# Where w_ch2 is converted, who makes w2's high parts, and a first MLP pass over two chunks

## The chip, the core and the metric

The kernel runs on one core of one Trainium2 chip. The metric is device time in microseconds (us), from the first to the last instruction. Lower is better. Three runs of the kernel before gave 1047.99, 1050.70 and 1052.57 us; the median is 1050.7 us.

## The reference, cut to what matters

Three stages follow one another: causal attention with a cumulative bias, a mixture of 8 experts (one expert for each token), and a mixer with a channel MLP. B=4, S=576, so 2304 tokens; the model width DM is 512.

```python
attn_out = _attn_ref(q, k, v, s)                   # 4 x 8 x 576 x 64
# experts: w1 is 8 x 512 x 1024, w2 is 8 x 1024 x 512, float32
h = np.maximum(x[b, s] @ w1[e], 0.0)
out[b, s] = p[e] * (h @ w2[e])
# mixer: U 576 x 32, V 32 x 576, w_ch1 512 x 2048, w_ch2 2048 x 512
h = xt @ U @ V
u = x + h.transpose(0, 2, 1)
ch = np.maximum(u @ w_ch1, 0.0) @ w_ch2
return (u + ch).astype(np.float32)
```

`w_ch1`, `w_ch2`, `U` and `V` arrive as float64. The kernel turns them into float32 on the chip by integer operations on their words.

## The kernel before, in words

Every product is made of three products of float32 parts: a number is split into a high part, which TensorE takes exactly, and a low part, and high by high, high by low and low by high are summed in PSUM. So each weight needs a high part (a cast) and a low part (a subtraction). The helper `conv` (L228) makes both: the high part on the engine it is given (GpSimd at L232, ScalarE at L236), the low part at L239.

The work is staged. Attention and the router come first, in an order written out by hand (`ORDER`); the change touches nothing there. Then come the experts, one after the other, by falling count of tokens, with 384, 384, 368, 336, 320, 304, 256 and 256 rows (`CAPS`); they are called experts 0 to 7 here. The mixer and the MLP come last, over 9 chunks of 256 tokens.

Experts and MLP share the loop `ffn` (L1512). One step f of it holds 12 matmuls of the first product into a PSUM tile `ps_h` (L1524), ScalarE's relu `hh` (L1501) and VectorE's low part `hl` (L1502), and then, `skew` steps late, the second product of an earlier step into `acc` (L1538): 3 matmuls for each 128 tokens. After each step a `hook` issues the work that stands beside the loop. The experts have 8 steps with a skew of 2, so 10 hooks each and 80 in all (NH = 10). The MLP has 16 steps with a skew of 1.

The order of every engine's queue is the order of the program text, so a hook decides what stands in front of what. An expert's hook issues, in this order:
- `mix_step` (L1881): for each tile of 128 rows of the expert before, a cast `yh`, a subtraction `yl` (L1939) and 3 matmuls into `pu` (L1853).
- `run_convs` (L1832): step f converts `w1` unit f of the next expert (high part on ScalarE, low part on VectorE) and `w2` unit f-2 (both parts on GpSimd). The units overwrite a ring of 16 tiles that the present expert still reads, so a unit of `w2` waits for the last `acc` matmul on the old one.
- `load_raws` (L1828): the loads for the hook after next, on SP, into a pool of 5 buffers.
- the rows of the next expert (`load_x` L1757, indirect DMAs on GpSimd; `trans_x` L1773 on TensorE, L1776; `split_x` L1779), and `ug_make` (L1789, GpSimd, L1804).
- one entry of a list `seq` (L1839 to L1848, popped at L1914): the conversions of float64 weights. A unit of 128 x 512 is a 512 KB load on SP, an absolute value on ScalarE (L256), three tensor_scalar on VectorE (L257, L265, L273), two scalar_tensor_tensor on VectorE (L285, L293), and a use. Each unit takes two entries.

`seq` holds 16 units of `w_ch2` first, then 16 of `w_ch1`, then 2 of `V`: 70 entries, one of them before the loop and one in each hook after it. The use of a `w_ch2` unit is a store of its float32 words to DRAM (`c2_d`, L1470). The use of a `w_ch1` unit is the high part on ScalarE (L1455) and the low part on GpSimd (L1456), into tiles that stay. In the hooks of expert 7, where no next expert's weights are due, `run_convs` loads the 16 units of `c2_d` back (`load_c2` L220) and splits them into the ring: 15 with ScalarE and VectorE, one on GpSimd.

After the experts, the last rows are scattered to DRAM (`yt_d`, L1926), and the MLP's first chunk is prepared: its rows are loaded (L2004), the mixer's product is made (`ph`, L2018) and added (L2025), and the sum is transposed (`ups`, L2032) and split into `uh` (L2034) and `ul` (L2035). These PSUM tiles come from a ring of two. The next chunk is prepared inside the loop of the present one: its hooks 8 and 10 make the sums, 11 and 13 the transposes.

Of the kernel before, what the change touches and what calls it, by code (L numbers as in the profile page):

```python
# [12 lines left out]
F32 = mybir.dt.float32  # L13
# [14 lines left out]
# the order of issue of the attention's and the router's jobs  # L28
# [99 lines left out]
def kernel(  # L128
# [37 lines left out]
    # rows that the main path takes of the first expert, then of the others by falling count  # L166
# [19 lines left out]
    # rows of all tokens; those of the first expert by place; what else a place needs  # L186
# [7 lines left out]
    c2_d = dram.tile([F2, DM], F32, name="c2_d")  # L194
# [114 lines left out]
    # ------------------------------------------------------------------  # L309
    # causal attention with the cumulative bias, and the router  # L310
    # ------------------------------------------------------------------
    with ExitStack() as ax:
# [240 lines left out]
        # ---- v as two float16 parts, a column of ones beside each head; the v of a pair of  # L553
        # heads is scaled by a power of two first, by the sum of its magnitudes ----
# [14 lines left out]
        # for each pair of heads: what scales v, and the power of two to undo it  # L569
# [778 lines left out]
        def group_jobs(g):  # L1348
            """Loads of four heads."""
# [91 lines left out]
    # V as its high part twice and its low part, for a product with the parts of U' x stacked  # L1441
# [20 lines left out]
    def c2_job(pool, f):  # L1462
# [6 lines left out]
        def use(t):  # L1469
            nc.sync.dma_start(c2_d[f * P : (f + 1) * P], t)  # L1470
# [41 lines left out]
    def ffn(ps1, psa, hpool, xh, xl, n, u1, u2, nf, skew, hook):  # L1512
        rows = [(i, min(P, n - i * P)) for i in range((n + P - 1) // P)]
        acc = [psa.tile([P, DM], F32, tag=f"acc{i}", name=f"acc{i}") for i, _ in rows]
        done = []
        for f in range(nf + skew):
            if f < nf:
# [3 lines left out]
                ops = [(wh, xh), (wh, xl), (wl, xh)]  # L1521
                for kk in range(KD):
# [211 lines left out]
    with ExitStack() as mx:  # L1734
# [141 lines left out]
        for g_ in seq.pop(0):  # L1876
            g_()
# [252 lines left out]
```

## Time and profile before

| what | value |
|---|---|
| median of 3 runs | 1050.7 us |
| span of the profiled execution | 1056.8 us |
| TensorE busy over the span | 91% |
| VectorE, ScalarE, GpSimd busy | 56%, 38%, 39% |
| mean granted clock of TensorE | 0.952 |
| first matmul of experts 0 to 7 at | 329.2, 366.25, 403.95, 440.96, 477.27, 515.95, 555.79, 592.97 us |
| first matmul of the MLP at | 631.12 us |

The profiled execution's own time is its span, as the page gives it; it is 6.1 us above the median of the timed runs. "Busy" counts the time in which an engine had an instruction under way, and says nothing of whether that instruction was waiting for something inside it. A matmul's end is modelled and matmuls overlap, so the pace of TensorE is read from how many matmuls lie between two points of time, not from their single durations. The granted clock is given in parts of 2.4 GHz.

### The profile page before, as it was taken

The numbers are of one execution on the slowest core, as the hardware profiler recorded it, in microseconds if no ns is written. First come the engines' busy times: TensorE is split into PE (matmuls) and PEld (weight loads), VectorE is DVE, ScalarE is ACT, GpSimd is POOL, SyncE is SP. The second block draws the span as 40 slices with busy tenths as digits, with TensorE's granted clock in tenths as the row PEclk, the third lists the DMA queues.
The fourth block names the chain that finished last, engine by engine and source line by source line (L and its number), as shares of the span: only waits on it lengthen the run. The fifth ranks groups of instructions, "written<-read, shape, count | busy, mean of one in ns | idle before, by whom it ended". The sixth has DMA issues, their size and how long they took to land.

```text
span 1056.8 us, 19123 instructions
## 1 busy us (share of the span) xinstructions
PE 964.1 (91%) x7139; PEld 853.1 (81%) x7139; DVE 590.3 (56%) x1136; ACT 406.6 (38%) x960; POOL 410.3 (39%) x508
## 2 busy tenths in 40 slices
PE   5888998889847999998897879999999999999998
PEld 4777887778746988887686759999999999999997
DVE  6676887767745888989999851222222222222221
ACT  4676877777622334435444341111111111111111
POOL 6633636355643877889999920000000000000000
PEclk9898999999956999999998989999999999999999
DMA  7998998967126697677575450101010100101000
GB/s 171 196 204 158 233 216 209 213 134 177 35 73 192 223 309 246 211 258 220 172 214 179 135 181 1 35 6 41 1 40 1 40 21 21 40 1 41 1 20 20
DMA packets 132132, 129.25 MB, mean 122 GB/s; under 512 B 59015, under 2 KB 100295, under 8 KB 130240
## 3 DMA queue, kind: packets, MB, share of 16 engines
q1 hardware_dynamic: 123968, 114.03, 40.0%
q0 software_dynamic: 6864, 13.63, 4.4%
q8 instruction: 58, 0.95, 0.4%
q10 hardware_dynamic: 1200, 0.30, 0.1%
q14 instruction: 42, 0.34, 0.1%
HBM read 81.04 MB, written 26.49 MB: 102 GB/s over the span
## 4 chain that ended last, share of the span: by engine, by line
PE 59%; POOL 13%; DMA 8%; DVE 7%; issue 6%; SPq 4%; ACT 3%; POOLq 0%; DVEq 0%; ACTq 0%
PE ps_h L1524 24%; PE acc L1538 22%; POOL ring L239 4%; DMA OP<-parts 3%; PE pp L779 3%; POOL ring L232 2%; POOL c1u L1456 2%; SPq L541 2%; PE ob L828 2%; PE sm L1012 1%; PE sp L709 1%; PE sp L716 1%; POOL ug L1804 1%; DMA OP<-b_d 1%; POOL yt_d L1926 1%
## 5 line engine op out<-in xcount | busy, mean ns | idle before, releaser
L1538 PE MATMUL acc<-ring,hh 128*128 128x512 f32 x928 | 291.6, 395 | 0.0
L1502 DVE SCALAR_TENSOR_TENSOR hl<-ps_h,hh 128x256 fp32r<-128x256 f32 (+5 forms) x208 | 92.3, 444 | 288.7 <-ACT hh L1501 285.7
L1501 ACT ACTIVATE hh<-ps_h 128x256 fp32r<-128x256 f32 (+5 forms) x208 | 83.3, 400 | 415.8 <-PE ps_h L1524 400.8
L1524 PE MATMUL ps_h<-uh,c1u 128*128 128x256 f32 x1152 | 232.1, 286 | 0.7 <-ACT uh L2034 0.7
L1524 PEld LDWEIGHTS ps_h<-uh,c1u 128*128 128x128 f32 x1152 | 190.0, 192 | 6.1 <-ACT uh L2034 1.1
L1538 PE MATMUL acc<-ring,hl 128*128 128x512 f32 (+4 forms) x464 | 181.7, 392 | 1.9 <-DVE hl L1502 1.9
L1538 PEld LDWEIGHTS acc<-ring,hh 128*128 128x128 f32 x928 | 161.1, 187 | 25.8
L1524 PE MATMUL ps_h<-ul,c1u 128*128 128x256 f32 x576 | 164.1, 285 | 0.1
L1524 PE MATMUL ps_h<-xh,ring 128*128 128x384 f32 (+5 forms) x512 | 128.1, 322 | 2.8 <-DVE hl L1502 2.2
L1524 PEld LDWEIGHTS ps_h<-ul,c1u 128*128 128x128 f32 x576 | 110.9, 193 | 5.1 <-DVE ul L2035 0.4
L1538 PEld LDWEIGHTS acc<-ring,hl 128*128 128x128 f32 (+4 forms) x464 | 85.9, 185 | 24.1 <-DVE hl L1502 2.7
L792 DVE SCALAR_TENSOR_TENSOR lo<-pp,hi 128x384 f16<-128x384 f32 (+2 forms) x160 | 85.3, 549 | 24.7 <-ACT hi L787 19.6
L1524 PEld LDWEIGHTS ps_h<-xh,ring 128*128 128x128 f32 x512 | 92.8, 197 | 6.6 <-DVE hl L1502 2.8
L239 POOL TENSOR_TENSOR ring<-raw_out,ring 128x512 fp32r<-128x512 f32 x60 | 88.2, 1470 | 5.0
L779 PE MATMUL pp<-ident,Pb 128*128 128x128 f32 x480 | 83.9, 297 | 6.1 <-DVE lo L792 2.3
L787 ACT ACTIVATE hi<-pp 128x384 f16<-128x384 f32 (+2 forms) x160 | 77.0, 496 | 32.1 <-PE pp L779 25.2
L1524 PE MATMUL ps_h<-xl,ring 128*128 128x384 f32 (+5 forms) x256 | 82.3, 322 | 1.6 <-DVE xl L1782 1.5
L750 ACT ACTIVATE Pb<-sp,nm 128x192 f32<-128x192 f32 (+4 forms) x160 | 80.8, 535 | 6.8 <-DVE nm L733 5.7
L709 PE MATMUL sp<-OP 128*128 128x288 f32 (+4 forms) x192 | 71.6, 377 | 8.5 <-DMA OP<-parts 2.8
L733 DVE TENSOR_REDUCE nm<-sp 128x1 f32<-128x576 f32 (+4 forms) x96 | 67.5, 703 | 15.9 <-PE sp L724 13.8
L828 PE MATMUL ob<-VP,hi 128*128 128x65 f16 x960 | 59.1, 199 | 5.8 <-ACT xr L840 5.7
L716 PE MATMUL sp<-OP 68*128 68x288 f32 (+4 forms) x192 | 60.7, 321 | 2.8 <-DMA OP<-b_d 2.8
(228 smaller groups left out, 1579.7 us busy)
## 6 DMA issues: line engine op xcount, KB each, us to landing
raw_in<-in_moe_w_dram SPq DMA_DIRECT2D x64, 256.0 KB
raw_out<-in_moe_w_dram SPq DMA_DIRECT2D x64, 256.0 KB
raw<-in_moe_w_ch_dram SPq DMA_DIRECT2D x32, 512.0 KB
OP<-parts SPq DMA_DIRECT2D x28, 576.0 KB
OP<-parts SPq DMA_DIRECT2D x28, 288.0 KB
out_dram<-ut SPq DMA_DIRECT2D x9, 512.0 KB
kn<-in_k_dram SPq DMA_DIRECT2D x32, 128.0 KB
x_d<-x SPq DMA_DIRECT2D x16, 256.0 KB
```

What stands on the lines that cost most here:

```text
L239: lo_eng.tensor_tensor(out=lo, in0=src, in1=hi.bitcast(F32), op=ALU.subtract)
L709: nc.tensor.matmul(sp[:, c, :cw], lhsT=W1[j][:, h, t * P : (t + 1) * P], rhs=K1[j][:, h, c0 : c0 + cw], start=True, stop=False,)
L716: nc.tensor.matmul(sp[:, c, :cw], lhsT=W2[j][0:SK, h, t * P : (t + 1) * P], rhs=K2[j][0:SK, h, c0 : c0 + cw], start=False, stop=not diag,)
L750: nc.scalar.activation(out_, in_, AF.Exp, scale=-1.0, bias=k["nm"][:, x : x + 1])
L779: nc.tensor.transpose(pp[:, i - i0], k["pb"][:, a, x * P : (x + 1) * P], ident)
L787: nc.scalar.activation(k["hi"][:, i0:i1], k["pp", i0][:, : i1 - i0], AF.Copy, scale=SCALE)
L792: nc.vector.scalar_tensor_tensor(out=k["lo"][:, i0:i1], in0=k["pp", i0][:, : i1 - i0], scalar=SCALE, in1=k["hi"][:, i0:i1], op0=ALU.mult, ...
L828: nc.tensor.matmul(o[:, h], lhsT=pt[:, a * (t + 1) + x], rhs=VP[n % 2][:, z, x, h], start=(x == 0 and i == 0), stop=(x == t and i == len(t ...
L1501: nc.scalar.activation(hh[:, :n], ps[:, :n], AF.Relu)
L1502: nc.vector.scalar_tensor_tensor(out=hl[:, :n], in0=ps[:, :n], scalar=0.0, in1=hh[:, :n].bitcast(F32), op0=ALU.max, op1=ALU.subtract,)
L1524: nc.tensor.matmul(ps[:, :n], lhsT=wa[:, kk], rhs=xa[:, kk, :n], start=(kk == 0 and i == 0), stop=(kk == KD - 1 and i == 2),)
L1538: nc.tensor.matmul(acc[i][0:m], lhsT=ha[:, sl], rhs=u2[g][:, wa], start=(g == 0 and jj == 0), stop=(g == nf - 1 and jj == 2),)
```

## The change

What it does:
- The store to `c2_d` and the loads back are gone. A unit of `w_ch2` is now split straight from the converted words (high part on ScalarE, low part on GpSimd).
- The `w_ch2` units leave the experts' list. `seq` holds 16 units of `w_ch1` and 2 of `V`: one entry before the loop, and 37 spread evenly over the first 68 hooks, all within experts 0 to 6. The list of `w_ch2` has 34 entries: one in each of the 10 hooks of expert 7, and then two in each hook of the MLP's first pass until it is empty.
- The high parts of `w2` for experts 1 to 7 go from GpSimd to ScalarE. Their low parts stay on GpSimd.
- The MLP's first pass takes two chunks (512 tokens): each step makes 24 matmuls of 256 columns into one `ps_h` tile, one relu and one `hl` of 512 columns, and 12 `acc` matmuls. Both chunks are prepared ahead of the pass. The other 7 chunks run as before.
- Buffers: the conversions' tiles are in a pool of their own that outlives the experts, `mixb` is in the pool of raw weights, `ut`, `uh` and `ul` have 3 buffers for 2, and `hh` and `hl` have skew + 1 buffers.

The diff, without the comments that it drops:

```diff
-    c2_d = dram.tile([F2, DM], F32, name="c2_d")
...
-    def load_c2(f):
-        raw = wraw.tile([P, DM], F32, tag="raw", name="raw_c2")
-        nc.sync.dma_start(raw, c2_d[f * P : (f + 1) * P])
-        return raw
...
         def use(t):
-            nc.sync.dma_start(c2_d[f * P : (f + 1) * P], t)
+            conv(c2u[f], t, False, nc.scalar, nc.gpsimd)
...
-    def ffn(ps1, psa, hpool, xh, xl, n, u1, u2, nf, skew, hook):
+    def ffn(ps1, psa, hpool, xs, n, u1, u2, nf, skew, hook, names=None):
...
+                for x, (xh, xl) in enumerate(xs):
+                    ops = [(wh, xh), (wh, xl), (wl, xh)]
+                    for kk in range(KD):
+                        for i, (wa, xa) in enumerate(ops):
+                            nc.tensor.matmul(
+                                ps[:, x * cut : (x + 1) * cut],
+                                lhsT=wa[:, kk],
+                                rhs=xa[:, kk, :cut],
+                                start=(kk == 0 and i == 0),
+                                stop=(kk == KD - 1 and i == 2),
+                            )
+                done.append(relu_split(hpool, ps, n, wide, skew + 1))
...
+    fj = ctx.enter_context(tc.tile_pool(name="fj", bufs=1, reuse_waits="tile"))
...
                 else:
-                    a = (w1u[f], lambda f=f: load_c2(f), False)
-                    b = (w2u[f], lambda f=f: load_c2(f + NF), False)
+                    continue
                 convs.setdefault(e * NH + f, []).append((a, nc.scalar, nc.vector))
-                swift = (nc.scalar, nc.vector)
-                slow = (nc.gpsimd, nc.gpsimd)
-                here = swift if e + 1 == E and f + 1 < NF else slow
-                convs.setdefault(e * NH + f + 2, []).append((b, *here))
+                convs.setdefault(e * NH + f + 2, []).append((b, nc.scalar, nc.gpsimd))
...
-        jobs = [c2_job(m3, f) for f in range(NF2)]
-        jobs += [c1_job(m3, f) for f in range(NF2)]
-        jobs += [v_job(m3, half) for half in range(2)]
...
+        seq = in_turn(
+            [c1_job(fj, f) for f in range(NF2)] + [v_job(fj, half) for half in range(2)]
+        )
+        seq_c2 = in_turn([c2_job(fj, f) for f in range(NF2)])
+
+        gaps = (E - 1) * NH - 2
+        seq_at = {}
+        for i, x in enumerate(seq[1:]):
+            seq_at.setdefault(i * gaps // (len(seq) - 1), []).extend(x)
...
-                if seq:
-                    for g_ in seq.pop(0):
+                for g_ in seq_at.pop(g, ()):
+                    g_()
+                if e + 1 == E:
+                    for g_ in seq_c2.pop(0):
                         g_()
...
-            m = c3.tile([P, DM], F32R, tag="mixb", name="mixb", bufs=2)
+            m = wraw.tile([P, DM], F32R, tag="raw", name="mixb")
...
+        spans = [[0, 1]] + [[c] for c in range(2, NCH)]
...
+        for c in spans[0]:
+            at[c] = start_chunk(c)
+            for part in range(2):
+                for i in range(CH // P):
+                    prepare(c, i, part)
+        for n, cs in enumerate(spans):
+            ahead = spans[n + 1] if n + 1 < len(spans) else []
...
+                if n == 0:
+                    if f == 0:
+                        low_mix()
+                    for _ in range(2):
+                        if seq_c2:
+                            for g_ in seq_c2.pop(0):
+                                g_()
...
+            names = [f"acc{i % 2}" for i in range(len(cs) * CH // P)]
+            acc = ffn(
+                ps1, psa, c3, [at[c][2:] for c in cs], CH * len(cs), c1u, c2u, NF2, 1, hook,
+                names,
+            )
```

## Rows read from the trace of the kernel before

**Rows 1.** The page, its part on the chain that ended last: shares by engine.

```profile
PE 59%; POOL 13%; DMA 8%; DVE 7%; issue 6%; SPq 4%; ACT 3%; POOLq 0%; DVEq 0%; ACTq 0%
```

**Rows 2.** Windows: stretch, its length, busy us (instructions) by engine, clock, DMA share, GB/s.

```profile
329.20:440.96 111.76, 110.35 (x559) 98.62 (x560) 92.67 (x135) 44.99 (x86) 83.85 (x92) 0.98 0.74 243
440.96:477.27 36.31, 35.18 (x191) 30.16 (x190) 32.94 (x48) 15.75 (x31) 29.82 (x31) 1.00 0.77 246
477.27:515.95 38.68, 35.87 (x190) 30.34 (x189) 37.33 (x46) 17.50 (x35) 36.23 (x36) 0.96 0.67 209
515.95:555.79 39.84, 35.53 (x187) 28.95 (x186) 38.91 (x47) 17.75 (x34) 37.71 (x37) 0.96 0.66 199
555.79:592.97 37.18, 29.29 (x163) 24.35 (x161) 34.67 (x48) 16.96 (x34) 35.04 (x33) 0.91 0.57 178
592.97:620.20 27.23, 24.66 (x151) 21.28 (x149) 19.16 (x30) 13.90 (x28) 16.50 (x19) 1.00 0.56 183
620.20:631.10 10.90, 5.46 (x16) 3.06 (x16) 4.62 (x9) 4.53 (x9) 4.42 (x4) 0.66 0.39 137
631.10:1056.80 425.70, 420.57 (x2674) 381.18 (x2674) 100.63 (x205) 64.69 (x160) 0.00 (x0) 0.99 0.06 21
```

**Rows 3.** The chain in order of time: start, duration, engine, tile and line.

```profile
348.39 2.10 PE ps_h L1524 x12
350.50 2.08 PE acc L1538 x9
...
394.51 0.87 PE xps L1776 x8
...
413.89 0.70 PE pu L1853 x3
...
638.65 1.43 PE ps_h L1524 x12
640.09 1.39 PE acc L1538 x6
```

**Rows 4.** Single lines between 515.95 and 592.97 us: count, shortest/median/longest ns, first, last.

```profile
L239 POOL TENSOR_TENSOR ring<-raw_out,ring x17: 1292/1591/1622, 514.4 to 592.5; 128x512 fp32r<-128x512 f32 x17
L232 POOL TENSOR_SCALAR ring<-raw_out x16: 617/792/1057, 517.6 to 591.8; 128x512 fp32r<-128x512 f32 x16
L1456 POOL TENSOR_TENSOR c1u<-t,c1u x10: 1303/1468/1742, 515.9 to 584.2; 128x512 fp32r<-128x512 f32 x10
L1804 POOL TENSOR_TENSOR ug<-u,sd x10: 398/582/850, 549.8 to 591.2; 128x128 fp32r<-128x128 f32 x10
L239 DVE TENSOR_TENSOR ring<-raw_in,ring x16: 675/841/2323, 524.6 to 591.8; 128x512 fp32r<-128x512 f32 x16
L285 DVE SCALAR_TENSOR_TENSOR t<-t,l x9: 679/978/1652, 520.3 to 586.1; 128x512 int32<-128x512 int32 x9
L293 DVE SCALAR_TENSOR_TENSOR t<-raw,t x10: 692/1658/2590, 514.8 to 587.2; 128x512 int32<-128x512 int32 x10
L1939 DVE TENSOR_TENSOR yl<-y,yh x6: 674/836/2131, 523.3 to 573.3; 128x512 fp32r<-128x512 f32 x4, 64x512 fp32r<-64x512 f32 x1, 48x512 fp32r<-48x512 f32 x1
```

**Rows 5.** Groups by line and shape: count, busy us, mean ns, idle before and its releasers.

```profile
L236 ACT CAST ring<-raw_in 128x512 fp32r<-128x512 f32 x56 | 34.5, 617 | 26.6 <-DMA raw_in<-in_moe_w_dram 26.0 <-issue 0.5
L273 DVE TENSOR_SCALAR t<-t 128x512 int32<-128x512 int32 x34 | 24.4, 718 | 1.2
L1502 DVE SCALAR_TENSOR_TENSOR hl<-ps_h,hh 128x256 fp32r<-128x256 f32 x160 | 67.6, 423 | 270.9 <-ACT hh L1501 270.9
```

**Rows 6.** Waits from 325 to 640 us: who for whom, us in total, times, longest.

```profile
ACT hh L1501 <- PE ps_h L1524: 75.9, 33, 4.6
```

**Rows 7.** Timeline around the start of the MLP: start, duration, engine, line, operation.

```profile
627.73 1.37 DVE L2025 TENSOR_TENSOR ut<-ph,ut 128x512 f32<-128x512 f32 x2 [1.68 <-DMA ut<-yt_d]
630.30 1.49 DVE L2035 TENSOR_TENSOR ul<-ups,uh 128x512 fp32r<-128x512 f32 x2 [1.20 <-ACT uh L2034]
631.12 0.58 PE L1524 MATMUL ps_h<-uh,c1u 128*128 128x256 f32 x1 [0.68 <-ACT uh L2034]
```

More of the change, by code (lines that the diff above doesn't have):

```diff
@@ L1510, in relu_split @@
         return hh, hl
-    def ffn(ps1, psa, hpool, xh, xl, n, u1, u2, nf, skew, hook):
+    def ffn(ps1, psa, hpool, xs, n, u1, u2, nf, skew, hook, names=None):
         rows = [(i, min(P, n - i * P)) for i in range((n + P - 1) // P)]
-        acc = [psa.tile([P, DM], F32, tag=f"acc{i}", name=f"acc{i}") for i, _ in rows]
+        names = names or [f"acc{i}" for i, _ in rows]
+        acc = [psa.tile([P, DM], F32, tag=names[i], name=names[i]) for i, _ in rows]
+        cut = n // len(xs)
+        wide = len(xs) * xs[0][0].shape[2]
         done = []
@@ L1520, in ffn @@
                 wl = unit_view(u1[f], 1, True)
-                ops = [(wh, xh), (wh, xl), (wl, xh)]
-                for kk in range(KD):
-                    for i, (wa, xa) in enumerate(ops):
-                        nc.tensor.matmul(
-                            ps[:, :n],
-                            lhsT=wa[:, kk],
-                            rhs=xa[:, kk, :n],
-                            start=(kk == 0 and i == 0),
-                            stop=(kk == KD - 1 and i == 2),
-                        )
-                done.append(relu_split(hpool, ps, n, xh.shape[2]))
+                for x, (xh, xl) in enumerate(xs):
[10 more added lines that the diff above has]
+                done.append(relu_split(hpool, ps, n, wide, skew + 1))
             g = f - skew
@@ L1875 @@
         load_raws(1)
-        for g_ in seq.pop(0):
+        for g_ in seq[0]:
             g_()
@@ L1958 @@
         nc.scalar.copy(al.bitcast(F32), pu)
-        run_convs(E * NH - 1)
-        while seq:
-            for g_ in seq.pop(0):
-                g_()
-        assert not raws
+        assert not raws and not seq_at
     ux.close()
@@ L1999, in mix @@
         def mix(c):
-            ut = c3.tile([P, CH // P, DM], F32, tag="ut", name="ut", bufs=2)
+            ut = c3.tile([P, CH // P, DM], F32, tag="ut", name="ut", bufs=3)
             cut = CH // P if c == 0 else 1
@@ L2047, in start_chunk @@
             ut, one = mix(c)
-            uh = c3.tile([P, KD, CH], F32R, tag="uh", name="uh", bufs=2)
-            ul = c3.tile([P, KD, CH], F32R, tag="ul", name="ul", bufs=2)
+            uh = c3.tile([P, KD, CH], F32R, tag="uh", name="uh", bufs=3)
+            ul = c3.tile([P, KD, CH], F32R, tag="ul", name="ul", bufs=3)
             return ut, one, uh, ul
-        cur = start_chunk(0)
-        for i in range(CH // P):
-            cur[1](i)
-        for i in range(CH // P):
-            trans_u(cur[0], i, cur[2], cur[3])
@@ L2057 @@
-        for c in range(NCH):
-            ut, _, uh, ul = cur
-            box = {}
-            def hook(f, c=c, box=box):
-                if c == 0 and f == 1:
-                    low_mix()
-                if c + 1 == NCH:
-                    return
-                if f == 4:
-                    box["n"] = start_chunk(c + 1)
-                if f in (8, 10):
-                    box["n"][1]((f - 8) // 2)
-                if f in (11, 13):
-                    trans_u(box["n"][0], (f - 11) // 2, box["n"][2], box["n"][3])
-            acc = ffn(ps1, psa, c3, uh, ul, CH, c1u, c2u, NF2, 1, hook)
-            for i in range(CH // P):
-                nc.vector.tensor_tensor(
-                    out=ut[:, i], in0=acc[i], in1=ut[:, i], op=ALU.add
-                )
-            nc.sync.dma_start(
-                out.rearrange("b s d -> (b s) d")[c * CH : (c + 1) * CH].rearrange(
-                    "(i p) d -> p i d", p=P
-                ),
-                ut,
-            )
-            cur = box.get("n")
+        spans = [[0, 1]] + [[c] for c in range(2, NCH)]
@@ new lines, with prepare, hook @@
+        at = {}
+        def prepare(c, i, part):
+            ut, one, uh, ul = at[c]
+            if part == 0:
+                one(i)
+            else:
+                trans_u(ut, i, uh, ul)
+        for c in spans[0]:
[5 more added lines that the diff above has]
+            ahead = spans[n + 1] if n + 1 < len(spans) else []
+            def hook(f, n=n, ahead=ahead):
+                if n == 0:
[5 more added lines that the diff above has]
+                                g_()
+                if f == 4:
+                    for c in ahead:
+                        at[c] = start_chunk(c)
+                for c in ahead:
+                    if f in (8, 10):
+                        prepare(c, (f - 8) // 2, 0)
+                    if f in (11, 13):
+                        prepare(c, (f - 11) // 2, 1)
+            names = [f"acc{i % 2}" for i in range(len(cs) * CH // P)]
[3 more added lines that the diff above has]
+            )
+            for x, c in enumerate(cs):
+                ut = at.pop(c)[0]
+                for i in range(CH // P):
+                    nc.vector.tensor_tensor(
+                        out=ut[:, i], in0=acc[x * (CH // P) + i], in1=ut[:, i], op=ALU.add
+                    )
+                nc.sync.dma_start(
+                    out.rearrange("b s d -> (b s) d")[c * CH : (c + 1) * CH].rearrange(
+                        "(i p) d -> p i d", p=P
+                    ),
+                    ut,
+                )
@@ L2087 @@
+        assert not seq_c2
 _INS = [
```

31 lines of the change are left out of this document (16 added, 15 removed).

## The prediction

> **What bounds the kernel now.** I read the page's chain first, then windows cut at each expert's first matmul, then the chain in order of time for TensorE's pace, then single lines of the crowded stretch. TensorE holds 59% of the chain, GpSimd 13% [rows 1]. GpSimd does nothing in the MLP [rows 2], so its share must be somewhere in the experts.
>
> Each expert's length is to be compared with what TensorE needs for it. At full clock 12 first-product matmuls of 384 columns take 2.10 us and of 256 columns 1.43 us; I interpolate the others: 2.02 at 368 rows, 1.85 at 336, 1.77 at 320, 1.68 at 304. Second-product matmuls take 2.08 us for 9 and 1.39 for 6, a tile's `pu` 0.70, two tiles' transposes 0.87 [rows 3]. With 8 steps, three tiles of `pu` from the expert before and the next expert's transposes (two or three tiles):
> - experts 0 to 2: 34.7 + 36.8 + 36.2 = 107.7 us; they took 111.8
> - expert 3: 8 x 3.93 + 2.1 + 1.3 = 34.8; it took 36.3
> - expert 4: 8 x 3.85 + 3.4 = 34.2; 38.7
> - expert 5: 8 x 3.76 + 3.0 = 33.1; 39.8
> - expert 6: 8 x 2.82 + 3.0 = 25.5; 37.2
> - expert 7: 22.6 + 1.4 (two tiles of `pu`, no transposes) = 24.0; 27.2 [rows 2].
>
> So the excess is 4.1, 1.5, 4.5, 6.7, 11.7 and 3.2: 31.7 us in all, 23 of it in experts 4 to 6. There VectorE and GpSimd are both busy for 90 to 98% of the stretch, while ScalarE is busy for less than half [rows 2]. The `w_ch1` units, which alone use GpSimd, come only in these experts, since 16 `w_ch2` units stand in front of them.
>
> How the two engines bound it is seen in durations. In experts 5 and 6 the same VectorE operation on two SBUF tiles takes 0.69 us or 2.59, and a GpSimd one 1.29 or 1.62 [rows 4]. Suppose that these never run at the same time and each needs its shortest duration. GpSimd: 17 x 1.29 + 16 x 0.62 + 10 x 1.30 + 10 x 0.40 = 48.9 us. VectorE: 16 x 0.68 + 9 x 0.68 + 10 x 0.69 + 6 x 0.67 = 27.9. The sum, 76.8, is the 77.0 us that the two experts took. I take this sum as their bound.
>
> The Trainium skill, "SBUF — State Buffer", section "Who interferes with whom", says that a VectorE instruction with two SBUF inputs and a GpSimd instruction that reads SBUF exclude each other, and that ScalarE never waits for either. The trace agrees as far as the stretched durations and the sum show. Without that rule expert 6 would be worth 2 us more below (25.5 for 27.7).
>
> The MLP is bound by TensorE: 420.6 of 425.7 us busy, at clock 0.99 [rows 2].
>
> **The change, part by part.** The profiled execution's span is 1056.8 us, 6.1 above the median of 1050.7; its page shows nothing around the span. I take the difference in us from the profile and set it against the median.
>
> (a) Casts of `w2`. 56 casts of at least 0.62 us leave GpSimd, 8 for each next expert [rows 4]. On ScalarE each costs 0.62 [rows 5], so 5 us per expert: busy time rises from about 17.8 to 22.7 of 33 us in expert 5. ScalarE has that room: relus waited 75.9 us for `ps_h` [rows 6]. The move adds a wait: the cast needs the `acc` matmul that frees the tile, and behind it on ScalarE stand a `w_ch1` cast, an absolute value and the next `hh`. The next `hh` can't begin before the next 12 matmuls, 1.4 to 2.1 us later, and its product is due two steps later; I cost it at nothing, and its price if that cover is gone is a rival.
>
> (b) `w_ch2` leaves experts 0 to 6, and `w_ch1` and V spread over 68 hooks. VectorE loses 5 operations for each of 16 units, SP 16 loads of 512 KB and the stores that waited for VectorE. GpSimd keeps its 16 `w_ch1` operations, but 2.7 per expert instead of 5. In experts 5 and 6 the sum above loses 16 x 0.62 = 9.9 (casts), 4.6 x 1.30 = 6.0 (GpSimd's `w_ch1`) and 4.1 x 1.37 = 5.6 (VectorE's two operations): 55.3 us, or 27.7 each. Expert 5 is then bound by TensorE (33.1), expert 6 by the pair (27.7). I allow 0.8 for expert 5 and 0.5 for expert 6 at their borders, about what experts 1 to 3 lose now. New lengths: expert 3 35.3 (-1.0), expert 4 35.0 (-3.7), expert 5 33.9 (-5.9), expert 6 28.2 (-9.0); experts 0 to 2 -0.8 in all, since most of their excess is the first matmuls at a lower clock.
>
> (c) Expert 7. The 16 loads from `c2_d` on SP, 15 casts, 15 subtractions on VectorE and one unit on GpSimd go; the 16 stores that SP issued in experts 0 to 3 go too. In their place stand 10 entries: SP issues 7 loads of 512 KB, VectorE does five first halves and four second halves, GpSimd four low parts. With the crowded medians that is 5 x 2.2 + 4 x 2.6 = 22 us on VectorE, with the two last operations at their shortest 5 x 2.2 + 4 x 1.37 = 16.5 [rows 4, 5]; beside it stand 3.4 of `hl` and 2.1 of `yl`, against 24 of TensorE. GpSimd is nearly free there, so the shortest are nearer, and VectorE just keeps up. I take an excess of 1.7 for 3.2: -1.5. Bounds: -3.2, or +3 if VectorE is late.
>
> (d) The first pass. TensorE's work is the same: each half of the pass loads its own weights. Per step it is 2 x 2.82 = 5.64 us. Beside it stands one `w_ch2` unit: three VectorE operations of about 0.72 [rows 5], the two others of 0.98 and 1.66 at their crowded medians [rows 4], and an `hl` below 0.85: 5.65 us. With those two at their shortest it is 4.4, which is nearer, since GpSimd has one operation a step. Unit f+4 is issued in hook f and read in step f+5, so it is ahead. ScalarE does a relu, an absolute value and a cast, some 2 us a step. SP's 512 KB a step find idle DMA engines (0.06 [rows 2]). Cost nothing. The bound from above is rival 3.
>
> (e) Both chunks ahead of the pass. From the first sum to the first matmul one chunk takes 631.12 - 627.73 = 3.4 us [rows 7]. The second waits for the first one's `ul`, because its PSUM tiles are the same two; so it adds some 3.4 us, at a clock of 0.66 [rows 2]. In return 8 transposes and two `ph` matmuls (0.87 + 2 x 0.23 = 1.3) leave the loop. Net +2.1; bounds -1.3 (all covered) and +5.5 (the chain twice, less 1.3, should that low clock last longer).
>
> (f) Buffers, `low_mix` one hook earlier, four sums at the end of the first pass instead of two (0.69 each, beside 2.8 us of first product): nothing, with the MLP's idle VectorE as cover.
>
> Sum: -0.8 - 1.0 - 3.7 - 5.9 - 9.0 - 1.5 + 2.1 = -19.8 us. From the profile's 1056.8 that is 1037.0, and from the median **1030.9**, so 1031.
>
> **The rivals.**
> 1. Less of it: VectorE still serves `hl`, `xl` and `yl` late at the borders of experts, where its queue is deep. For: experts 1 to 3 lose time with GpSimd at 80%. Against: VectorE falls to about 25 us in 33. If half of the 18.6 us in experts 4 to 6 stays, the gain is 10.5: 1040; with (e) at its upper bound 1044.
> 2. All of it: the pair doesn't bound expert 6, nothing is lost at the borders, and the cold start alone stays (0.02 of clock over 111.8 us, 2.2). 31.7 - 2.2 - 2.1 = 27.4: 1023.
> 3. Conversion starves the first pass: load, ScalarE, VectorE, ScalarE and GpSimd follow one another, and a unit takes 9 us instead of 5.6. Twelve units take 108 us against the 93 that TensorE gives them: +15, so 1046. Against: two units are under way at once, and the loads have the DMA engines for themselves.
> 4. Slower: ScalarE's queue becomes the wait. In expert 6 a step is 2.82 us, and `hh`, two weight casts, a `w_ch1` operation and `yh` are 2.9. If each of the 56 casts holds TensorE up by its 0.62, that is +34.7 and the sum +14.9: 1066. It decides once a step's ScalarE work exceeds TensorE's step in most hooks. Against: only hooks with all five do, the two steps of skew absorb it, and ScalarE's mean would be 22 of 28 us.
>
> **How the numbers follow.** The forecast has 0.65, rival 1 0.17, rival 2 0.06, rival 3 0.06, rival 4 0.06. A measurement of this kernel can tell about 0.5% (5.3 us) from no change. Faster takes the forecast, rival 2 and 0.12 of rival 1; the same takes rival 3 and the rest of rival 1; slower is rival 4. That is 0.83, 0.11 and 0.06. The range leaves out rivals 3 and 4 and the tails: 1022, which is all of the excess gone with (e) costing little, to 1044, the upper end of rival 1.
>
> **What would show it.** Right: experts 4, 5 and 6 start 35.0, 33.9 and 28.2 us apart; GpSimd's busy share in them is below 0.9; VectorE's longest operations there shrink; no GpSimd cast of `w2` on the chain; the first MLP matmul comes some 5.5 us after the first sum instead of 3.4; the first pass takes 90 us. Wrong: `hh` waiting for nothing but ScalarE's own queue, `acc` in the first pass waiting for ScalarE or GpSimd, or expert 6 still over 33 us.

## The result, and the profile after

The changed kernel is faster by a little over 1%. Its 8 runs have a median of 1041.7 us (1037.1 to 1046.3), the 8 of before beside them 1052.0 (1047.2 to 1056.3); the ratio is 0.9894, 95% interval 0.9862 to 0.9927. Two more comparisons, each on one chip, gave 0.9865 (0.9819 to 0.9911) and 0.9888 (0.9853 to 0.9922). So the gain is 11 to 14 us, where 19.8 was forecast.

The start of the experts moved by itself, in stages that the change doesn't touch: it came 329.2 us after the start in both profiles of before, and 324.9, 327.4 and 330.3 us in the three of the changed kernel. So I compare from the experts' first matmul to the end: 727.6 and 725.6 us before, 712.3, 712.7 and 714.6 after, 13.4 us less in the mean. The spans of the two first profiles differ by 19.7 us, almost the 19.8 of the forecast; 4.3 of that is this earlier start, so the agreement is luck.

The changed kernel's page, its chain by engine (for [rows 1]):

```profile
PE 75%; DMA 8%; DVE 5%; SPq 4%; issue 3%; ACT 2%; POOL 2%; POOLq 0%; ACTq 0%; DVEq 0%
```

GpSimd's 13% have become 2. The changed kernel's windows, cut at the same events as [rows 2] (experts 0 to 7, the transition, the first pass of two chunks, the rest), with the same columns:

```profile
324.85:361.62 36.77, 35.24 (x181) 31.54 (x181) 24.64 (x32) 16.45 (x31) 23.54 (x26) 1.00 0.69 208
361.62:400.83 39.21, 37.24 (x190) 33.09 (x189) 28.08 (x38) 21.07 (x39) 25.29 (x26) 1.00 0.60 193
400.83:438.24 37.41, 36.17 (x191) 32.06 (x189) 27.49 (x37) 19.51 (x37) 25.16 (x26) 1.00 0.50 156
438.24:475.77 37.53, 35.56 (x191) 30.10 (x190) 28.86 (x37) 20.48 (x39) 26.09 (x26) 1.00 0.64 197
475.77:511.54 35.77, 34.55 (x191) 29.08 (x189) 24.97 (x35) 19.99 (x39) 27.91 (x26) 1.00 0.65 203
511.54:545.43 33.89, 33.47 (x186) 27.48 (x185) 26.62 (x39) 19.78 (x38) 24.75 (x24) 1.00 0.57 180
545.43:573.27 27.84, 26.95 (x162) 22.48 (x160) 19.45 (x30) 16.24 (x33) 23.44 (x25) 1.00 0.61 180
573.27:598.83 25.56, 24.53 (x151) 21.54 (x150) 17.99 (x33) 10.16 (x21) 13.12 (x14) 1.00 0.35 123
598.83:615.07 16.24, 8.70 (x27) 5.21 (x27) 8.87 (x14) 6.65 (x12) 3.27 (x3) 0.66 0.39 124
615.07:707.79 92.72, 92.72 (x590) 84.64 (x588) 53.91 (x86) 24.92 (x43) 15.54 (x12) 0.99 0.20 63
707.79:1037.10 329.31, 324.39 (x2078) 294.02 (x2076) 77.17 (x158) 50.06 (x124) 0.00 (x0) 1.00 0.08 25
```

Against the forecast, term by term (us, from the first profile of each):

| stretch | before | forecast | after |
|---|---|---|---|
| experts 0 to 2 | 111.8 | 111.0 | 113.4 |
| expert 3 | 36.3 | 35.3 | 37.5 |
| expert 4 | 38.7 | 35.0 | 35.8 |
| expert 5 | 39.8 | 33.9 | 33.9 |
| expert 6 | 37.2 | 28.2 | 27.8 |
| expert 7 | 27.2 | 25.7 | 25.6 |
| transition and MLP | 436.6 | 438.7 | 438.3 |

Experts 5, 6 and 7 and the MLP came out as forecast. Experts 0 to 4 did not: they are 5.4 us longer than forecast, and experts 1 to 3 are longer than before, by 1.5, 0.4 and 1.2 us. The waits show why. The changed kernel, from the experts' first matmul to the MLP's (who for whom, us in total, times, longest):

```profile
ACT ring L230 <- PE acc L1537: 63.8, 45, 1.7
...
PE xps L1776 <- issue: 6.1, 5, 1.2
```

ScalarE's cast of `w2` (now L230) waits for the `acc` matmul, 45 times, and TensorE has a new wait of 1.2 us in front of the third transposed tile, five times. The same moment in the timelines of ScalarE and TensorE, at the end of expert 0 (start, duration, line, operation, idle before):

```profile
355.84 0.62 ACT L230 CAST ring<-raw_out 128x512 fp32r<-128x512 f32 x1 [1.59 <-PE acc L1537]
356.37 0.62 ACT L230 CAST ring<-raw_in 128x512 fp32r<-128x512 f32 x1
356.89 1.06 ACT L1781 CAST xh<-xps 128x512 fp32r<-128x512 f32 x2
```

```profile
357.46 0.39 PE L1537 MATMUL acc<-ring,hl 128*128 128x512 f32 x1
359.08 0.63 PE L1776 MATMUL xps<-ident,xrow 128*128 128x128 f32 x4 [1.24 <-issue]
```

The transposed tiles use a ring of two in PSUM. The third can't be made before the first is split by ScalarE (`xh`) and VectorE (`xl`). Both splits now stand behind the `w2` cast: ScalarE's in its own queue, and VectorE's behind a subtraction that waits for ScalarE's cast of `w1`, which follows the `w2` cast. VectorE at the same moment:

```profile
357.02 1.37 DVE L233 TENSOR_TENSOR ring<-raw_in,ring 128x512 fp32r<-128x512 f32 x1 [2.18 <-ACT ring L230]
358.31 1.27 DVE L1782 TENSOR_TENSOR xl<-xps,xh 128x512 fp32r<-128x512 f32 x2
```

ScalarE is done with both splits at 357.95. It is the first `xl`, begun at 358.31, that ends just before the transpose starts at 359.08. Before, the wait was the other way round: in such a place ScalarE idled 2.6 us until the third transposed tile came.

The transition takes 16.2 us for 11.0. Of this, 3.2 us is the second chunk: its product `ph` waits for the first one's `ul` until 611.87, and its last transpose is under way at 615.07, when the MLP begins. The rest is at the start of the transition. TensorE's rows, and then ScalarE after the last `acc` matmul, which ended at 598.83:

```profile
602.36 0.70 PE L1859 MATMUL pu<-yh,ug 128*128 128x512 f32 x2 [3.53 <-ACT yh L1946]
...
611.87 1.65 PE L2022 MATMUL ph<-mix,vs 96*128 96x512 f32 x2 [0.55 <-DVE ul L2039]
...
615.07 0.56 PE L1523 MATMUL ps_h<-uh,c1u 128*128 128x256 f32 x1
```

```profile
599.38 0.62 ACT L230 CAST ring<-t 128x512 fp32r<-128x512 f32 x1 [3.10 <-DVE t L287]
...
600.47 1.24 ACT L1931 ACTIVATE y<-acc,sd 128x512 f32<-128x512 f32 x2
```

A unit of `w_ch2` waits there for VectorE, and the last rows' scaling `y` stands behind it. `pu` begins 3.5 us after the last `acc` matmul; before it was 1.4.

### The profile page after: what moved, and what is told of

It is laid out like the page before. It is cut to its first block, busy times and chain, and to the rows that moved or that the text cites. A ratio compares the mean times of both kernels' runs of the same rounds, so it can differ in the third digit from the quotient of the medians.

```text
span 1037.1 us, 19005 instructions
## 1 busy us (share of the span) xinstructions
PE 956.5 (92%) x7139; PEld 846.3 (82%) x7139; DVE 568.4 (55%) x1105; ACT 435.0 (42%) x1001; POOL 375.1 (36%) x466
## 3 DMA queue, kind: packets, MB, share of 16 engines
q1 hardware_dynamic: 119360, 105.64, 38.6%
## 4 chain that ended last, share of the span: by engine, by line
PE 75%; DMA 8%; DVE 5%; SPq 4%; issue 3%; ACT 2%; POOL 2%; POOLq 0%; ACTq 0%; DVEq 0%
PE ps_h L1523 30%; PE acc L1537 29%; DMA OP<-parts 3%; PE pp L773 3%; SPq L535 2%; PE ob L822 2%; DMA OP<-b_d 2%; PE sp L703 2%; PE sp L710 1%; PE pu L1859 1%; PE sm L1006 1%; PE ups L2036 1%; PE xps L1776 1%; PE xtp L993 1%; SPq L440 1%
## 5 line engine op out<-in xcount | busy, mean ns | idle before, releaser
L1496 DVE SCALAR_TENSOR_TENSOR hl<-ps_h,hh 128x256 fp32r<-128x256 f32 (+6 forms) x192 | 89.9, 468 | 253.4 <-ACT hh L1495 252.9
L1523 PE MATMUL ps_h<-uh,c1u 128*128 128x256 f32 x1152 | 228.4, 284 | 0.0
L1495 ACT ACTIVATE hh<-ps_h 128x256 fp32r<-128x256 f32 (+6 forms) x192 | 80.8, 421 | 340.9 <-PE ps_h L1523 340.6
L1537 PEld LDWEIGHTS acc<-ring,hh 128*128 128x128 f32 x928 | 161.5, 186 | 27.2 <-ACT hh L1495 0.5
L1523 PE MATMUL ps_h<-xh,ring 128*128 128x384 f32 (+5 forms) x512 | 123.6, 313 | 0.7 <-ACT xh L1781 0.7
L233 POOL TENSOR_TENSOR ring<-raw_out,ring 128x512 fp32r<-128x512 f32 x60 | 81.4, 1361 | 53.0 <-ACT ring L230 52.3
L786 DVE SCALAR_TENSOR_TENSOR lo<-pp,hi 128x384 f16<-128x384 f32 (+2 forms) x160 | 85.2, 549 | 19.8 <-ACT hi L781 18.9
L1523 PEld LDWEIGHTS ps_h<-xh,ring 128*128 128x128 f32 x512 | 88.6, 188 | 4.4 <-ACT xh L1781 1.5
L1523 PE MATMUL ps_h<-xl,ring 128*128 128x384 f32 (+5 forms) x256 | 80.1, 313 | 2.5 <-DVE xl L1782 2.5
L233 DVE TENSOR_TENSOR ring<-raw_in,ring 128x512 fp32r<-128x512 f32 x56 | 51.7, 922 | 42.5 <-ACT ring L230 42.3
L230 ACT CAST ring<-raw_out 128x512 fp32r<-128x512 f32 x60 | 37.0, 621 | 75.6 <-PE acc L1537 63.8
```

Source lines behind the costliest of these rows:

```text
L230: hi_eng.copy(hi, src)
L233: lo_eng.tensor_tensor(out=lo, in0=src, in1=hi.bitcast(F32), op=ALU.subtract)
L786: nc.vector.scalar_tensor_tensor(out=k["lo"][:, i0:i1], in0=k["pp", i0][:, : i1 - i0], scalar=SCALE, in1=k["hi"][:, i0:i1], op0=ALU.mult, ...
L1495: nc.scalar.activation(hh[:, :n], ps[:, :n], AF.Relu)
L1496: nc.vector.scalar_tensor_tensor(out=hl[:, :n], in0=ps[:, :n], scalar=0.0, in1=hh[:, :n].bitcast(F32), op0=ALU.max, op1=ALU.subtract,)
L1523: nc.tensor.matmul(ps[:, x * cut : (x + 1) * cut], lhsT=wa[:, kk], rhs=xa[:, kk, :cut], start=(kk == 0 and i == 0), stop=(kk == KD - 1 and ...
```

## The experiments

**e1: the changed kernel again**

> The changed kernel as it is, a second time. From the experts' start to the end its first profile was 15.4 us shorter than that of before (712.2 for 727.6), while the timed medians lay only 10.3 us apart. If the profile of before happened to be a slow execution, the ratio stays near 0.989 (1041 us). If the timed runs were disturbed, it goes to 0.985 (1036 us). In either case the third transposed tile of experts 0 to 4 again waits 1.2 us, five times, and the transition to the MLP takes 16 us instead of 11.

1041.8 us, ratio 0.9865 (0.9819 to 0.9911). The five waits and the long transition (16.0 us) were there again, and so were experts 1 to 7 to within 0.1 us each. The gain lies between the two readings; the next run settles which side was odd.

**e8: before again**

> Before, a second profile. If its first profile was a usual execution, the time from the experts' first matmul to the end is again 725 to 729 us with experts 4 to 6 at 38 to 40 us each. If it was an unlucky one, experts 4 to 6 come out 3 us or more shorter in all.

725.6 us from the experts' start, experts 4 to 6 at 38.1, 39.9 and 37.5 us. So the first profile of before was a usual one, and the excess read from it was there to win.

**e2: only the casts**

```diff
                 here = swift if e + 1 == E and f + 1 < NF else slow
+                if e + 1 < E:
+                    here = (nc.scalar, nc.gpsimd)
```

> Before, with the casts of w2 for experts 1 to 7 on ScalarE and nothing else changed. Theory (VectorE and GpSimd exclude each other, and the cast on ScalarE makes the transposes wait): experts 5 and 6 lose 16 x 0.62 = 9.9 us of their sum of 76.8, expert 4 some 4, and five borders gain 1.2 us of wait each: -8 us, 1044. Rival (GpSimd's own time is the bound, with casts at their mean of 0.82): 56 x 0.82 us less on GpSimd, of which experts 4 to 6 get 19: experts 4 to 6 go to TensorE's pace, -20 us, 1032. Second rival (the casts bring nothing, the w_ch2 move does all): 1052.

1056.4 us beside 1056.7: ratio 0.9981 (0.9945 to 1.0018). The casts alone bring nothing that can be measured; the theory's -8 us is missed, and the second rival held. The profile is of an execution of 1060.9 us, the third longest of 12, so it tells where the time went in that one. Windows of experts 3 to 6:

```profile
442.20:482.99 40.79, 36.68 (x191) 31.20 (x189) 34.96 (x49) 21.98 (x41) 27.51 (x26) 0.96 0.70 221
482.99:523.19 40.20, 36.18 (x190) 30.10 (x189) 36.69 (x48) 22.59 (x43) 30.56 (x28) 0.96 0.65 201
523.19:557.59 34.40, 34.10 (x187) 27.34 (x185) 34.02 (x41) 20.95 (x40) 27.03 (x25) 1.00 0.72 228
557.59:597.42 39.83, 30.75 (x162) 25.28 (x161) 37.20 (x52) 20.96 (x41) 29.64 (x27) 0.88 0.64 187
```

GpSimd is far from full, and expert 5 gains 5.4 us against [rows 2], but experts 3, 4 and 6 lose 4.5, 1.5 and 2.6. Experts 5 and 6 took 74.2 us, where the exclusive sum less the casts is 66.9. All five borders have the wait before the third transpose; at the ends of experts 3 and 4 it was 3.8 and 4.0 us. There `xl` stood in VectorE's queue behind the first half of a `w_ch1` unit, at 1.4 to 1.5 us an operation, and a subtraction of 1.7 us.

**e4: the rest without the casts**

```diff
-                convs.setdefault(e * NH + f + 2, []).append((b, nc.scalar, nc.gpsimd))
+                convs.setdefault(e * NH + f + 2, []).append((b, nc.gpsimd, nc.gpsimd))
```

> The changed kernel with the w2 casts back on GpSimd, the rest as changed. Theory (sum of the exclusive operations): experts 5 and 6 have 55.3 + 9.9 = 65.2 us of them, 32.6 each, against TensorE's 33.1 and 25.5, so expert 6 grows by 5 us, expert 5 by 1; the five waits of 1.24 us go: within 2 us of the changed kernel, 1041. Rival (the casts' leaving GpSimd carries the gain): 10 us or more slower than the changed kernel, 1051 or over. Rival (the cast on ScalarE costs more than it brings): 4 us or more faster.

1040.7 us, ratio 0.9867 (0.9822 to 0.9912), the same as e1 on the same chip. Windows of experts 1 to 6:

```profile
363.85:401.10 37.25, 37.25 (x191) 33.06 (x189) 27.26 (x37) 15.59 (x31) 33.24 (x36) 1.00 0.64 201
401.10:437.07 35.97, 35.97 (x191) 32.15 (x189) 27.78 (x38) 15.80 (x32) 30.53 (x33) 1.00 0.52 166
437.07:471.96 34.89, 34.89 (x190) 30.23 (x189) 25.18 (x36) 16.10 (x32) 31.10 (x34) 1.00 0.68 207
471.96:506.98 35.02, 34.55 (x191) 29.06 (x189) 28.36 (x36) 15.98 (x32) 32.57 (x33) 1.00 0.65 197
506.98:542.56 35.58, 33.98 (x187) 27.41 (x185) 27.65 (x37) 15.64 (x31) 33.46 (x34) 1.00 0.60 175
542.56:577.66 35.10, 28.85 (x162) 23.71 (x160) 20.63 (x33) 11.61 (x25) 28.76 (x32) 0.95 0.51 162
```

This is both sides of the casts. With them back on GpSimd, experts 1 to 4 are 6.8 us shorter than in the changed kernel (143.1 for 149.9), now at TensorE's own pace, and experts 5 and 6 are 9.0 longer (70.7 for 61.7). On ScalarE the casts lose in experts 1 to 4, where TensorE is the bound, and win in experts 5 and 6. The exclusive sum gave 65.2 there and doesn't explain the other 5.5 us: in expert 6 GpSimd was busy for 28.8 of 35.1 us and VectorE for 20.6. What the trace shows besides is that GpSimd runs late: its last low part of `w2` for expert 5 ends 9.9 us after that expert's first matmul, and the one for expert 6 as late; in the changed kernel it is 2.4 and 3.5 us.

**e3: the split ahead of the casts**

```diff
                 mix_step()
+                if e + 1 < E:
+                    if f == NF - 2:
+                        box["ps"] = [trans_x(xrow[i]) for i in range(2)]
...
                 if g + 1 < E * NH:
                     run_convs(g)
```

> The changed kernel with one move: in an expert's hook the transposes and splits of the next expert's rows are issued ahead of the weight conversions, so that on ScalarE and VectorE they stand ahead of the w2 cast that waits for the acc matmul. Theory (that cast at the head of ScalarE's queue holds up the split, and so the third transpose): the five waits of 1.24 us go and some of the waits for xl with them: 6 to 8 us less than the changed kernel, 1034. Rival (the wait only moves, to the casts or to hl, since the same work is in the same queues): within 2 us of the changed kernel.

1042.7 us, ratio 0.9862 (0.9815 to 0.9909): no gain. The five waits are gone, and experts 2, 3 and 4 are 1.4 us shorter each, but expert 1 took 41.4 us and expert 5 37.5, with waits of 2.8 and 2.5 us for `xl`. VectorE at the first of them:

```profile
361.91 1.52 DVE L251 TENSOR_SCALAR l<-raw 128x512 uint32<-128x512 uint32 x1
363.35 1.50 DVE L259 TENSOR_SCALAR t<-t 128x512 f32<-128x512 f32 x1
364.89 1.37 DVE L267 TENSOR_SCALAR t<-t 128x512 int32<-128x512 int32 x1
366.18 0.68 DVE L1782 TENSOR_TENSOR xl<-xps,xh 128x512 fp32r<-128x512 f32 x1
```

The first half of a `w_ch1` unit stands ahead of the third tile's split, and its three operations took 1.4 to 1.5 us each. Where GpSimd has nothing under way they take 0.42, 0.42 and 0.43; here GpSimd ran four operations one after another beside them. The rival held: the wait moved.

**e5: no pair**

```diff
-        spans = [[0, 1]] + [[c] for c in range(2, NCH)]
+        spans = [[c] for c in range(NCH)]
```

> The changed kernel with every chunk of the MLP in a pass of its own; the w_ch2 units still two entries a hook, so one unit per step of 2.8 us instead of 5.6. Theory (the pair is what gives the conversion its time): the 12 units left take some 5 us each from load to low part, 60 us, and the acc matmuls of the first pass wait: it takes 60 us or more instead of 45, the transition gets 3.2 us shorter, in all 10 us slower than the changed kernel, 1051. Rival (VectorE needs only 3.9 us a unit beside a relu of 256 columns, and four units are ready): the first pass waits 2 us or less, and the kernel is the same or 2 us faster, since the second chunk is prepared inside the loop again.

1057.4 us, ratio 1.0038 (1.0000 to 1.0076), so the whole gain is gone: it is 15.6 us above the changed kernel's 1041.8 on the same chip (e1). The transition shrinks to 12.9 us, but the MLP takes 442.8 for 422.0. VectorE over one step of the first pass:

```profile
642.95 0.42 DVE L251 TENSOR_SCALAR l<-raw 128x512 uint32<-128x512 uint32 x1
644.30 1.02 DVE L259 TENSOR_SCALAR t<-t 128x512 f32<-128x512 f32 x1 [0.94 <-ACT t L250]
...
645.70 0.42 DVE L1496 SCALAR_TENSOR_TENSOR hl<-ps_h,hh 128x256 fp32r<-128x256 f32 x1
646.03 0.68 DVE L279 SCALAR_TENSOR_TENSOR t<-t,l 128x512 int32<-128x512 int32 x1
646.75 0.69 DVE L287 SCALAR_TENSOR_TENSOR t<-raw,t 128x512 int32<-128x512 int32 x1
647.36 0.42 DVE L251 TENSOR_SCALAR l<-raw 128x512 uint32<-128x512 uint32 x1
```

From one L251 to the next it is 4.41 us, 0.94 of it waiting for ScalarE, whose absolute value stands behind the cast of the unit before. A step of one chunk is 2.82 us. Twelve steps 1.6 us too long make 19 of the MLP's 20.8 us. The theory had the direction and the wrong wait: `acc` waited for `hl`, which stands in the same queue, and not for the weights. From 610 to 690 us:

```profile
PE acc L1537 <- DVE hl L1496: 9.8, 10, 1.5
```

In the pair the step is 5.64 us and the same ring fits.

**e6: the units one a hook**

```diff
-            seq_at.setdefault(i * gaps // (len(seq) - 1), []).extend(x)
+            seq_at.setdefault(i, []).extend(x)
```

> The changed kernel with the w_ch1 and V units one entry in each of the first 37 hooks, as dense as in the kernel before, and none after expert 3. Theory (removal of the w_ch2 units is the gain, not the spreading, as long as TensorE's own time in the first experts is longer than the sum of the exclusive operations, 34.3 us for 34.8 to 36.8): experts 0 to 3 grow by 1 to 2 us each, expert 6 shrinks from 27.8 to 26, experts 4 and 5 by 0.5: within 4 us of the changed kernel, 1043. Rival (the spreading is half the gain): experts 0 to 3 grow by 3 us or more each, 1052.

1041.2 us, ratio 0.9864 (0.9797 to 0.9932). Experts 0 to 3 took 39.9, 39.3, 38.9 and 37.9 us, 5.0 more than in the changed kernel; expert 6 took 26.8. Of the 5.0, 3.1 is in expert 0, where the granted clock was 0.92 for 1.00; the third profile of the changed kernel has 38.9 us there, at 0.93. The theory held, within 4 us of the changed kernel. With the casts on ScalarE, the spreading is worth nothing that these runs resolve.

**e10: the `w_ch2` units gone, nothing else in the experts** (e4's and e6's edits together)

```diff
-                convs.setdefault(e * NH + f + 2, []).append((b, nc.scalar, nc.gpsimd))
+                convs.setdefault(e * NH + f + 2, []).append((b, nc.gpsimd, nc.gpsimd))
...
-            seq_at.setdefault(i * gaps // (len(seq) - 1), []).extend(x)
+            seq_at.setdefault(i, []).extend(x)
```

> The changed kernel without its other two parts in the experts: the w2 casts on GpSimd, and the w_ch1 and V units one a hook in the first 37 hooks. Theory (sum of the exclusive operations): experts 0 to 3 now hold what experts 4 and 5 held before, 25.0 us on GpSimd and 14.3 of two-input operations on VectorE, 39.3 together against TensorE's 35 to 37, so experts 1 and 2 take 39 to 39.5 us; experts 4 to 6 have 25.1 and go at TensorE's pace, 34.5, 33.5 and 26.5. Sum of the eight within 3 us of the changed kernel's 274, 1043. Rival (the sum is a coincidence, TensorE sets the first experts): experts 1 and 2 at 37.3 and 36.0 as in e4, the eight 267 in all, 1034.

1044.5 us, ratio 0.9847 (0.9804 to 0.9890). Windows of experts 1, 2, 5 and 6:

```profile
367.76:408.59 40.83, 38.60 (x190) 34.53 (x189) 38.28 (x49) 18.68 (x36) 37.96 (x36) 0.96 0.67 203
408.59:448.89 40.30, 37.90 (x191) 33.46 (x190) 38.52 (x49) 18.62 (x37) 37.08 (x36) 0.96 0.67 206
...
521.67:555.60 33.93, 33.47 (x187) 27.47 (x185) 13.07 (x21) 12.07 (x25) 27.27 (x32) 1.00 0.57 172
555.60:581.52 25.92, 25.92 (x162) 22.78 (x161) 12.74 (x21) 11.14 (x24) 23.19 (x27) 1.00 0.69 210
```

This is the test of the exclusive sum in another place. The crowd of [rows 2]'s experts 4 and 5 (both engines over 0.9 busy, TensorE's clock at 0.96) was moved into experts 1 and 2, and they took 40.8 and 40.3 us where the sum gave 39 to 39.5 and TensorE needs 36.8 and 36.2. Expert 6, emptied, went at TensorE's pace. The eight took 274.9 us, as expected. So taking the `w_ch2` units out of experts 0 to 6, into expert 7 and the paired pass, is by itself worth what the change is worth. It takes their loads, and the stores to `c2_d`, out of these experts too; no run separates that from what VectorE gains.

**e7, e9, e11: further moves.** e7 is e3 with two more moves, and e9 puts the casts where they win:

```diff
+            g = i * gaps // (len(seq) - 1)
+            seq_at.setdefault(g + (g % NH == NF - 1), []).extend(x)
...
+                if e + 1 == E and f + 1 < NH:
                     for g_ in seq_c2.pop(0):
```

> Splits ahead of the conversions, as in e3; no unit of w_ch1 in the hook just before the third tile's split (it goes one hook later); and none of w_ch2 in the last hook of expert 7, so that nothing stands ahead of the scaling of the last rows on ScalarE. Theory (the two waits for xl in e3 are the first half of a unit that stands ahead of the third tile's split on VectorE; the 2.1 us longer start of the transition is a w_ch2 cast that waits for VectorE): experts 1 to 5 take 36.8, 36.2, 35.3, 34.5 and 33.5 us, the transition 14 instead of 16.2: 9 us less than the changed kernel, 1032. Rival (the work that is moved holds up something else, as it did in e3): experts 1 to 5 stay above 182 us in all, where TensorE needs 175.

1036.7 us, ratio 0.9831 (0.9773 to 0.9889). Experts 1 to 5 took 38.6, 36.0, 36.8, 34.4 and 35.1, together 180.8: between theory and rival. The transition took 14.8 us for 14. What was left were waits of 1.3 to 1.5 us before `pu`, for `yl` or `yh`, in experts 1, 3 and 5.

```diff
+                convs.setdefault(e * NH + f + 2, []).append(
+                    (b, nc.scalar if e >= 5 else nc.gpsimd, nc.gpsimd)
+                )
...
+                if e + 1 == E and f + 1 < NH:
```

> The changed kernel with the w2 casts on ScalarE only in the hooks of experts 5 and 6 and on GpSimd in those of experts 0 to 4, and no w_ch2 entry in the last hook of expert 7. Theory (the cast on ScalarE is worth 9 us in experts 5 and 6, where the exclusive sum is the bound, and costs 6 to 7 us in experts 1 to 4, where TensorE is): experts 1 to 6 take 37.3, 36.0, 34.9, 35.0, 33.9 and 27.8 us, the transition 14.8; from the experts' start to the end 705 us for 712.5 of the changed kernel: 1034. Rival (the experts' gains don't add, because a backlog of GpSimd runs from expert 4 into 5): experts 5 and 6 over 65 us together, 1039.

1039.6 us, ratio 0.9797 (0.9755 to 0.9840), 710.6 us from the experts' start. Experts 1 to 4 came as expected (37.3, 36.0, 35.8, 34.7), experts 5 and 6 did not (36.1 and 30.7, together 66.8): the rival held, and the transition took 15.5 us for 14.8. A backlog from expert 4 fits the trace: GpSimd's last low part for expert 5 ends 9.9 us after that expert's first matmul, as in e4. No run takes the backlog away alone.

```diff
-            seq_at.setdefault(i * gaps // (len(seq) - 1), []).extend(x)
+            seq_at.setdefault(i // 6 * NH + 1 + i % 6, []).extend(x)
```

> As e7 (splits ahead of the conversions, no w_ch2 entry in the last hook of expert 7), with the 37 entries of w_ch1 and V placed in hooks 1 to 6 of each expert, so that no unit's operations stand in VectorE's queue in the last three hooks and the first one, where the splits xl and yl are due. Theory (what is left above TensorE's time in e7 are yl and xl behind a unit's operations at the border): experts 1 to 6 take 36.9, 36.2, 35, 34.4, 33.6 and 27.3 us, and from the experts' start to the end 704 us for 709 in e7 and 712.5 of the changed kernel: 9 us less than e12. Rival (the density in hooks 1 to 6 brings the excess back inside the expert): above 709 us, within 4 us of e12.

e11, which is e7 with this placing in place of its own, took 1034.6 us, ratio 0.9765 (0.9735 to 0.9796).

> The changed kernel a third time, beside e11, for a comparison on one chip: 712 us from the experts' start to the end, and a ratio to before of 0.984 to 0.99.

The changed kernel beside it took 1046.1, ratio 0.9888 (0.9853 to 0.9922). So e11 gains twice as much, and the intervals are apart: 11.6 us between the medians, where 9 were expected. The windows of its expert 6 and its transition:

```profile
546.10:572.85 26.75, 26.27 (x162) 22.83 (x161) 13.54 (x22) 16.18 (x32) 19.25 (x23) 1.00 0.69 207
...
597.26:612.03 14.77, 8.40 (x26) 5.09 (x27) 7.11 (x11) 5.03 (x10) 2.17 (x2) 0.67 0.43 137
```

Experts 1 to 6 took 203.7 us, where the theory had 203.4; TensorE's own time was reckoned at 200.6 (36.8 + 36.2 + 34.8 + 34.2 + 33.1 + 25.5). From the experts' start to the end it was 700.8 us, 3 less than expected.

## Why the prediction was right, and where it was not

The direction and the range held, the mechanism in part, and the size did not. The forecast was a gain of 19.8 us, and 11 to 14 came: 1041.7 us is where rival 1 stood (1040, or 1044), not 1031. Yet rival 1's reason is not the cause. It left half of the 18.6 us in experts 4 to 6, and all but 0.4 of that came; the rest was lost at the borders of experts 0 to 4 and in the transition. Step by step, with 15.4 us between the first two profiles:

- **What bounds it** held in part. The exclusive sum was argued from one stretch, where it came out at 76.8 for 77.0 us. That it came so near is luck: its counts take in three operations that lie mostly outside the stretch (in [rows 4] GpSimd's first and last L239 and VectorE's first L293), and without them it is 73.5. e10 built the crowd again elsewhere and took 1.0 to 1.5 us more than the sum. But e4 took 70.7 where it gives 65.2, and e2 74.2 where it gives 66.9. So it serves as a lower bound, and was nearly met where both engines were busy for over 0.9 of the time.
- **Step (a)** failed: "I cost it at nothing". I named the next `hh` as what stands behind the cast, with two steps of slack. At an expert's end the splits of the next expert's rows stand behind it too, ScalarE's directly and VectorE's by way of the `w1` cast. They have no slack, because the third transpose needs its PSUM tile back, and VectorE's came last. Price: five waits of 1.2 us, 6.1 us in all. e2 put the cast alone into the kernel before, and five such waits came; e4 took the casts away, the waits went, and experts 1 to 4 gave 6.8 us back. e3 moved the splits ahead, and these waits went. This was rival 4's mechanism, at the borders alone and not in every hook.
- **Step (b)** came out in its numbers: experts 5 and 6 at 33.9 and 27.8 for 33.9 and 28.2. For expert 6 that is luck. The forecast had it bound by the pair, at 27.7, with 5.4 `w_ch1` units left in the two experts. Three stand there:

```profile
L1450 POOL TENSOR_TENSOR c1u<-t,c1u x3: 1331/1469/1752, 518.8 to 546.0; 128x512 fp32r<-128x512 f32 x3
```

With what does stand there, at the durations of the prediction, the sum is 49.0 us, 24.5 for each and less than TensorE's 25.5; GpSimd was busy for 23.4 of the 27.8 us and VectorE for 19.5. What made up the 2.3 us above TensorE's time was not tested. I had also put the casts' share first. e4 shows that the whole change gains as much without them, since what they win in experts 5 and 6 they lose in experts 1 to 4, and e2 that alone they gain nothing.
- **Step (c)** held in length (25.6 for 25.7). The bound "+3 if VectorE is late" came true after the expert's end: `y` waited behind a unit's cast, and `pu` began 2.1 us later. e7, with that entry left out, had the transition 1.4 us shorter.
- **Step (d)** held: the first pass took 92.7 us for 90.2 of TensorE's, with no wait for weights. What it is worth was not in the sum, since the pair as such has no cost to save; e5 shows 16 us. Rival 3 was right about the ring of ScalarE and VectorE, but it takes 4.4 us and not 9, and it bites at 2.8 us a step and not at 5.6.
- **Step (e)** came to 3.2 - 3.6 = -0.4 us for +2.1. The second chunk's chain was 3.2 us for 3.4. In return the first pass is 3.6 us shorter than the two it replaces (92.7 for 96.3), not 1.3. So the table's 438.3 for 438.7 is luck again: this step's miss and the 2.1 us of step (c) cancel. The sign "some 5.5 us after the first sum" was reckoned wrongly too. The 1.3 us are saved later, inside the loop, so the step's own terms give 6.8; it was 6.5 (608.60 to 615.07). As for the 3.6 us: before, the MLP's first 24 matmuls ran at the lower of the two clocks for 6.0 us, and now the clock is back 2.6 us after the first of them. I put that down to the second chunk's preparation, in which TensorE is at work. e5 fits: it prepares one chunk alone, and the lower clock lasts 6.7 us. The second profile of before has only 3.8, so the size stays open. The MLP's start in the changed kernel and in e5:

```profile
615.07:617.70 2.63, 2.63 (x14) 2.63 (x13) 1.38 (x2) 0.70 (x2) 0.00 (x0) 0.50 0.00 0
...
610.26:616.96 6.70, 6.56 (x27) 6.07 (x28) 3.32 (x6) 0.81 (x2) 0.00 (x0) 0.50 0.01 2
```

The timed gain is 11 to 14 us where the first two profiles differ by 15.4; with all five profiles it is 13.4.

## What to carry to other kernels

Before an operation is put on an engine with time to spare, look at what stands behind it in that engine's queue at the borders of a loop, not only inside it: a wait at the head of an in-order queue is paid by whatever has the least slack behind it. Where two engines stretch each other's operations, add up the shortest durations of both and compare the sum with the stage. A match is a candidate for the bound, to be tested by building the same crowd elsewhere, as e10 did; it is no promise that work taken from either engine helps, since e2 took 9.9 us off the sum and gained nothing. Conversions that crowd one stage can go into a later one if its step is longer than the conversion's own ring of engines; that ring was 4.4 us here, and doubling the step from 2.8 to 5.6 us made room for it.

## What had not been expected

VectorE's tensor_scalar, with a single SBUF input, was stretched beside GpSimd too: 1.4 to 1.5 us in e3 in place of 0.4, three in a row, beside GpSimd's subtractions. The mean of 0.72 us that the prediction used in step (d) [rows 5] was such a stretched one. I had counted only operations on two SBUF tiles into the exclusive sum. Experts 5 and 6 of the kernel before have 30 of the others, 12.5 us at their shortest; with them the sum would be well above the 77.0 us that the two took, so they are held only in part. How much, no run shows.
